# Hyena filter and maxout FFN: the filter's hidden units placed over all four 64x64 quarters of the array, and the first loop's tail reordered

## The chip, the cores and the metric

The kernel runs on one core of one Trainium2 chip. The metric is the device time of one execution in microseconds. The kernel before took 2319.61 us as the median of three runs (2316.99 to 2319.65). One more execution was profiled: it took 2315.53 us, and the profile spans 2313.7 us of it, from the first to the last instruction. All times of single steps below are from that profile, counted from the start of its span.

## The reference

Two blocks follow one another. The first forms a long filter from position embeddings and convolves it, by FFT, with the product of two inputs; the second is a maxout feed-forward network over every token.

```python
# block 1: batch 4, seq S = 12544, d_model 128, filter_order 64
h_mlp  = np.maximum(pos_emb @ w1, 0.0) @ w2      # (S,64)@(64,64), Relu, @(64,128)
h_filt = h_mlp * np.exp(-0.01 * np.arange(S))[:, None]
u = x * v
y = irfft(rfft(u, 2S) * rfft(h_filt, 2S), 2S)[:, :S]
attn = x * y
# block 2: 50176 tokens, d_ff 768
h   = maximum(maximum(t @ w1, t @ w2), t @ w3)   # t: the tokens of attn
out = h @ w_out
```

The window exp(-0.01 n) is zero in float32 beyond 82 x 128 positions, so only the first 82 blocks of 128 positions of the filter are computed (NH = 82, HH = 41).

## The kernel before, in words

The sequence is seen as 98 blocks of 128 positions. The transform is done in two steps: a matmul over the blocks (tables `f1q` for the inputs, `f1h` for the filter), then one over the 128 positions within a block. `NK` = 45 pairs of frequencies follow. Everything is float32. In the profile, one float32 matmul instruction leaves two records, each with its own weight load.

**Start.** Loads of the position embeddings (`posT`, into the memory that `specH` uses later), of `w1` and of small tables are issued on three queues. Meanwhile TensorE multiplies zeros (`warm_up`), and `window_back` (L306) turns the window around into `winr`.

**Relu units of the filter** (`mlp_in`, L318, and `mlp_out`, L329). 82 blocks of positions are held as two halves of 41: half h = 0 on partitions 0 to 63 of `pos`, half h = 1 on partitions 64 to 127. For a position within the block, `mlp_in` multiplies the 41 columns of a half (the stationary operand, 41 columns that stand 128 floats apart in memory) with `w1` (64 wide). The result of half h goes to PSUM partitions 64h to 64h + 40. So half 0 always works in the upper left quarter of the array (rows and columns 0 to 63) and half 1 in the lower right one. Sixteen positions make one call: eight even ones (r = 0, PSUM bank 0 of the tile) and then eight odd ones (r = 1, bank 1). Eight calls alternate between two PSUM tiles `pms`; after each, VectorE takes two instructions (L332) for Relu times window into `hs`, which lies in `spec`.

**First transforms** (`quad`, L847, through `first_halves`, L158). 16 quads transform the 64 filter units from `hs` with `f1h`, whose rows 0 to 40 and 64 to 104 hold the two halves of the table; 32 quads transform the input of the first batch. VectorE converts FFN weights beside them.

**The first loop** (L970). 48 steps pipeline the second transform of filter and batch 0, their product and the inverse transform; step s works on frequency pair s in `g_second`, s - 1 in `s_filter` and `g_swap`, s - 2 in `g_re`, `g_im`, `g_unfold`, and s - 3 in `g_third`. `g_third` ends with a copy by ScalarE (L569) and a store to the DRAM tile `zd` (L570). In the two steps after the last `g_second`, `u_first` (L400) starts the first transform of batch 1 for units 0 to 3, two calls for each unit, each with 16 records on TensorE, one ScalarE copy (L418) and two VectorE instructions (L420). After the loop come `fold` (L913: one transpose of a piece of `w_sb[0]` by TensorE, a copy by ScalarE, and two matmuls into `pl`) for six pieces, `u_turn` for units 4 and 5, and `u_first` for units 4 and 5.

**The FFN** then begins: `t_load` (L642) loads `zt` from `zd` on SyncE's queue, VectorE forms sums (L670, L671), `t_last` (L678) makes the tokens, and `up` and `down` run the FFN, with the convolution of the next batch spread in between. SyncE's queue is in order: in front of the first `zt` load stand the loads of `f4p` (L1022) and `sign` (L1024). Their tiles lie in memory that the pools of the first part held, and the `f4p` load waits until those are free. `eye` and `w_sb[0]`, which the folds read, are in the pool `pin` with `specH` and `w2x`.

Each engine takes its instructions in the order in which the program lists them.

Of the kernel before, what the change touches and what calls it, by code (L numbers as in the profile page):

```python
# [10 lines left out]
FP32 = mybir.dt.float32  # L11
# [5 lines left out]
P = 128  # L17
# [8 lines left out]
N1 = 90  # L26
NH = 82
HH = NH // 2
# [14 lines left out]
def tables(NB):  # L43
    S = P * N1
    k1 = np.arange(N1).reshape(2, N1 // 2).T.ravel()
    n = np.arange(NB)
    a = e(np.outer(n, k1 + 0.25) / N1)
    f1 = np.concatenate([a.real, a.imag], 1)
    up = e(np.outer(n + 0.5, k1 + 0.25) / N1)
    f1q = np.stack([np.concatenate([up.real, up.imag], 1), f1], 1)  # L50
    f1h = np.zeros((64 + HH, 2 * N1))
    f1h[:HH], f1h[64:] = f1[:HH], f1[HH:NH]
    f4 = np.stack([a.T.real, a.T.imag], 1) / S
    f4p = f4[::2].transpose(1, 0, 2).reshape(N1, NB // 2, 2).transpose(0, 2, 1)
    f4 = np.stack([up.T.real, up.T.imag], 1) / S
    f4s = f4[::2].transpose(1, 0, 2).reshape(N1, NB // 2, 2).transpose(0, 2, 1)
    f4q = np.stack([f4p, f4s * np.array([1, -1])[:, None]], 1)
    j, t = np.arange(64), np.arange(64)
    tw = (k1[:, None, None] + 0.25) / S
    half = []  # L60
    for r in range(2):
        s2 = (127 - 2 * t - r)[None, :, None]
        half.append(stacked(e(tw * s2 + j[None, None, :] * s2 / 128)))
    fwd = np.stack(half, 2)
    half = []
    for q in range(2):
        s2 = (2 * t + q)[None, None, :]
        half.append(stacked(e(-tw * s2 - j[None, :, None] * s2 / 128)))
    inv = np.stack(half, 2)
    both = np.stack([fwd, inv], 2)  # L70
    both = both.reshape(N1 // 2, 2, P, 2, 256).transpose(0, 2, 3, 1, 4)
    both = both.reshape(N1 // 2, P, 2, 512)
    j, t = np.arange(32), np.arange(32)
    quarter = [[], []]
    for v in range(2):
        for w in range(2):
            s2 = (63 - 2 * t - v)[None, :, None]
            quarter[0].append(stacked(e(tw * s2 + (2 * j + w)[None, None, :] * s2 / 128)))
            s2 = (2 * t + w)[None, None, :]
            quarter[1].append(stacked(e(-tw * s2 - (2 * j + v)[None, :, None] * s2 / 128)))  # L80
    quarter = np.stack([np.stack(q, 1) for q in quarter], 1)
    quarter = quarter.reshape(N1 // 2, 2, 2, 2, 2, 64, 64).transpose(0, 3, 5, 2, 1, 4, 6)
    quarter = quarter.reshape(N1 // 2, P, 2, 256)
    steps = np.zeros((N1 // 2 + LATE, P, 2, 256))
    steps[:N1 // 2, :, 0], steps[LATE:, :, 1] = quarter[:, :, 0], quarter[:, :, 1]
    f32 = np.float32
    return tuple(np.ascontiguousarray(t, f32) for t in (f1q, f1h, f4q, both, steps))
# [3 lines left out]
def kernel(  # L91
# [15 lines left out]
    nc = tc.nc  # L107
# [50 lines left out]
    def first_halves(ps, lhs, table, dst, copy):  # L158


        for i, a in enumerate(lhs):
            for r in range(2):
                for c in range(2):
                    nc.tensor.matmul(  # L164
                        ps[64 * c:64 * c + 64, 256 * i + r * N1:256 * i + (r + 1) * N1],
                        a[:, r, :], table[:, c * N1:(c + 1) * N1],
                        start=(i % 2 == 0 and r == 0), stop=True, skip_group_check=True)
        copy(dst, ps[:].rearrange("p (s m) -> p s m", m=256)[:, :, 0:2 * N1].rearrange(
            "p s (r k) -> p k r s", r=2))
# [76 lines left out]
    inp = ctx.enter_context(tc.tile_pool(name="inp", bufs=3))  # L246
    utp = ctx.enter_context(tc.tile_pool(name="utp", bufs=2))
    pro = ExitStack()
    pin = pro.enter_context(tc.tile_pool(name="pin", bufs=1))
    eye = pin.tile([P, P], FP32, name="eye")  # L250
    w_sb[0] = pin.tile([D, DFF], FP32, name="w_sb0")
    lwp = pro.enter_context(tc.tile_pool(name="lwp", bufs=3))
    fin = ExitStack()
    inp0 = fin.enter_context(tc.tile_pool(name="inp0", bufs=3))
# [12 lines left out]
    w2_in = sml.tile([P, D], FP32, name="w2_in")  # L267
    w2x = pin.tile([P, D], FP32, name="w2x")
    win = sml.tile([64 + HH, P], FP32, name="win")
    winT = sml.tile([P, 64 + HH], FP32, name="winT")  # L270
    winr = sml.tile([64 + HH, 2, 64], FP32, name="winr")
    back = sml.tile([P, 2, 64], FP32, name="back")
    f1h = sml.tile([64 + HH, 2 * N1], FP32, name="f1h")
    warm = sml.tile([P, 256], FP32, name="warm")
    nc.vector.memset(warm[:], 0.0)
    nc.vector.memset(win[:], 0.0)
# [18 lines left out]
    nc.gpsimd.dma_start(w2_in[0:FO], w2[:, :])  # L295
    nc.gpsimd.dma_start(w2_in[FO:P], w2[:, :])
    nc.gpsimd.dma_start(f1q[:], f1_d)
    nc.scalar.copy(winT[:, 0:64], warm[:, 0:64])

    def warm_up(n):  # L300

# [4 lines left out]
    def window_back():  # L306
        pw = fps.tile([P, 1024], FP32, tag="cv", name="pw", bufs=2)
        nc.tensor.transpose(pw[:, 0:64 + HH], win[:], eye[0:64 + HH, 0:64 + HH])
        nc.scalar.copy(winT[:], pw[:, 0:64 + HH])
        nc.tensor.matmul(pw[0:64 + HH, 512:512 + P], winT[:],  # L310
                         back[:].rearrange("p r t -> p (r t)"), start=True, stop=True)
        nc.scalar.copy(winr[:].rearrange("n r t -> n (r t)"), pw[0:64 + HH, 512:512 + P])

    def w2_order():
# [3 lines left out]
    def mlp_in(i):  # L318

        ps = pms[i % 2]  # L320
        for r in range(2):
            for q in range(8):
                for h in range(2):
                    nc.tensor.matmul(  # L324
                        ps[64 * h:64 * h + HH, 512 * r + q * FO:512 * r + (q + 1) * FO],
                        posv[64 * h:64 * h + 64, P - 1 - 2 * (8 * i + q) - r, :],
                        w1_sb[64 * h:64 * h + 64], start=(q == 0), stop=True,
                        skip_group_check=True)
# [518 lines left out]
    def quad(lhs, table, dst):  # L847
        ps = fps.tile([P, 1024], FP32, tag="cv", name="ps1")
        first_halves(ps, lhs, table, dst, nc.scalar.copy)
# [16 lines left out]
    mps.close()  # L866
    fps = fin.enter_context(tc.tile_pool(name="fps", bufs=4, space=PSUM))
    for f in range(0, FO, 4):
        quad([hs[:, f + i] for i in range(4)], f1h[:], specH[:, :, :, f:f + 4])
        u, k = divmod(f // 4, 4)  # L870
        if u < 2:
            if k in (0, 1):
                u_mul(2 * u + k)
            if k == 2:
                turn2(2 * u)
                for v in range(2 * u + 6, 2 * u + 8):
                    u_load(0, v)
        some(2 if u < 2 and k < 2 else 3)
    wf = {g: load_dir(g, 0) for g in range(3)}
    wi = {g: load_dir(g, 1) for g in range(3)}  # L880
    for u in range(0, NU, 2):
        t = uts.pop(u)
        for v in range(2):
            if u + 4 < NU:
                u_mul(u + 4 + v)
            at = 4 * (u + v)
            quad([t[:, 4 * v + i] for i in range(4)], f1, spec[:, :, :, at:at + 4])
            some(1)
        if u + 4 < NU:
            turn2(u + 4)  # L890
        for v in (u + 10, u + 11):
            if v < NU:
                u_load(0, v)
        some(2)
# [25 lines left out]
    def s_minus(g):  # L920

        m = cvp.tile([P, 2, FO], FP32, tag="minus", name="minus", bufs=1)
        nc.gpsimd.tensor_single_scalar(m[:], specH[:, 2 * g:2 * g + 2, 0], -1.0, op=ALU.mult)
        minus[g] = m
# [41 lines left out]
    loads = dict(zip((NK - 16, NK - 14, NK - 12, NK - 9, NK - 8, NK - 4), range(EARLY)))  # L966
    muls = dict(zip((NK - 13, NK - 11, NK - 10, NK - 5, NK - 3, NK - 1), range(EARLY)))
    turns = {NK - 9: 0, NK - 4: 2}
    s_minus(0)
    for s in range(NK + 3):  # L970
        if s < NK:
            ws[s, 0] = wf[s]
            s_second(s)
            if s + 1 < NK:
                s_minus(s + 1)
            g_second(s)
            wf.pop(s)
            if s + 3 < NK:
                wf[s + 3] = load_dir(s + 3, 0)
        if 1 <= s <= NK:  # L980
            g_swap(s - 1)
            s_filter(s - 1)
        if s >= 3:
            ws[s - 3, 1] = wi.pop(s - 3)
            g_third(s - 3)
            if s < NK:
                wi[s] = load_dir(s, 1)
        if 2 <= s <= NK + 1:
            g_re(s - 2)
            g_im(s - 2)  # L990
            g_unfold(s - 2)
        if s < NK:
            g_butterfly(s)

        if s in muls:
            u_mul(muls[s])
        if s in turns:
            u_turn(turns[s])
            u_turn(turns[s] + 1)
        if s in loads:  # L1000
            u_load(1, loads[s])
        if NK <= s < NK + 2:
            for v in range(4):
                u_first(2 * (s - NK) + v // 2, 2 * (v % 2), 2)
    folded = [fold(0)]
    u_turn(4)
    u_turn(5)
    for f in range(1, NF):
        folded.append(fold(f))
        folded.pop(0)()  # L1010
    folded.pop()()
    nc.scalar.copy(lin[:], pl[:, 0:D])
    for u in (4, 5):
        for h in range(2):
            u_first(u, 2 * h, 2)
    pro.close()


# [153 lines left out]
```

## Time and profile before

| What (us of the span) | before |
|---|---|
| runs: median (lowest to highest) | 2319.61 (2316.99 to 2319.65) |
| span of the profiled execution | 2313.7 |
| TensorE busy, share of the span | 2277.5, 98% |
| `mlp_in` on TensorE, 512 records | 19.2 to 39.3 |
| first record of the filter's quads | 40.8 |
| last `g_third` on TensorE | 314.09 to 316.07 |
| `f4p` load issued / first `zt` load issued | 320.83 / 321.80 |
| first VectorE sum on `zt` | 326.44 |
| stretches at half clock | about 19.4 to 22.8, 313.0 to 316.4, 326.7 to 333.5 |

A line of the profile's groups names the line of the code, the engine, the operation, output and inputs by the program's names, the shapes, and the count; then come busy time, mean duration in nanoseconds, and the idle time of the engine in front of those instructions with what ended it. PE is TensorE's matmuls, PEld its weight loads, DVE VectorE, ACT ScalarE, POOL GpSimd; a name with q is an engine's queue for DMAs. The chain of waits goes back from the last instruction, at each step to what released it. TensorE's ends are modelled: what is measured well is the rate at which records follow each other.

### The profile page before, as it was taken

What the parts mean: (1) busy time and instruction counts of PE and PEld (TensorE: products, weight loads), DVE (VectorE), ACT (ScalarE), POOL (GpSimd) and SP (SyncE); (2) the same over time, 40 slices, a digit from 0 to 9 for tenths busy, and PEclk for the clock granted to TensorE, in tenths of its full rate; (3) what the DMA queues carried; (4) which work ended last, traced back from release to release, by engine and by line L of the source; (5) the groups of instructions that cost most, each with busy time, mean ns of one, the idle gap of its engine ahead of it and who ended that gap; (6) DMA issues with size and microseconds to landing.
All of it is one profiled execution on the core that took longest, in us unless ns stands there. A gap on an engine that the chain in (4) does not pass through costs nothing.

```text
span 2313.7 us, 68365 instructions
## 1 busy us (share of the span) xinstructions
PE 2277.5 (98%) x27853; PEld 1379.8 (60%) x27853; DVE 1574.2 (68%) x2856; ACT 1177.5 (51%) x2124; POOL 898.8 (39%) x1095
## 2 busy tenths in 40 slices
PE   8999989999999999999999999999999999999998
PEld 7989866655555546655555446655555546666665
DVE  5678856667887847757888847758888854445443
ACT  2678844446666624446666634446666632222222
POOL 1045424413333324423333333423333326666666
PEclk9999999999999999999999999999999999999999
DMA  7869959979998849979999849969999832222221
GB/s 158 206 202 266 290 155 189 166 172 246 232 244 216 210 119 192 185 147 242 248 243 250 214 120 189 186 144 247 247 246 240 225 91 56 54 56 71 65 55 22
DMA packets 473148, 410.95 MB, mean 178 GB/s; under 512 B 328004, under 2 KB 374231, under 8 KB 472834
## 3 DMA queue, kind: packets, MB, share of 16 engines
q1 hardware_dynamic: 433714, 317.68, 62.4%
q0 software_dynamic: 26400, 75.72, 11.2%
q10 hardware_dynamic: 12720, 13.18, 1.8%
q8 instruction: 219, 3.59, 0.7%
q14 instruction: 95, 0.78, 0.1%
HBM read 262.77 MB, written 84.67 MB: 150 GB/s over the span
## 4 chain that ended last, share of the span: by engine, by line
PE 84%; DMA 6%; ACT 3%; DVE 3%; issue 2%; SPq 1%; ACTq 1%; POOL 0%; DVEq 0%; POOLq 0%
PE hps L155 41%; PE ops L155 17%; PE ops L765 6%; PE cps L409 5%; PE cps L155 4%; PE cps L463 3%; PE ps L164 3%; PE cps L473 2%; DMA ht<-hd 2%; PE last L155 1%; DMA hd<-ht 1%; ACT ht L958 1%; DMA wt<-wq_const 1%; PE pm L324 1%; DMA zt<-zd 1%
## 5 line engine op out<-in xcount | busy, mean ns | idle before, releaser
L155 PE MATMUL hps<-gt,w_sb 128*64 128x392 f32 x6144 | 1150.4, 495 | 6.1 <-DVE hid L705 5.3
L702 ACT ACTIVATE hid<-hps 128x392 f32<-128x392 f32 x768 | 383.9, 500 | 736.6 <-PE hps L155 720.7
L155 PEld LDWEIGHTS hps<-gt,w_sb 128*64 128x64 f32 x6144 | 424.5, 137 | 437.4 <-issue 391.3
L705 DVE TENSOR_TENSOR hid<-hid,hps 128x392 f32<-128x392 f32 x768 | 427.3, 557 | 333.6 <-PE hps L155 323.9
L155 PE MATMUL ops<-hid,wo_sb 128*64 128x392 f32 x2304 | 478.6, 492 | 0.0
L515 POOL TENSOR_TENSOR cb<-cb,xs 128x512 f32<-128x512 f32 x135 | 181.7, 1346 | 471.4 <-DVE xs L512 331.1
L155 PEld LDWEIGHTS ops<-hid,wo_sb 128*64 128x64 f32 x2304 | 169.0, 137 | 210.2 <-issue 210.2
L488 DVE TENSOR_TENSOR cb<-cps,eo 128x512 f32<-128x512 f32 (+1 forms) x288 | 175.1, 649 | 65.6 <-ACT eo L485 65.1
L420 DVE TENSOR_TENSOR spec<-cps,high 128x360 f32<-128x360 f32 x180 | 135.5, 794 | 121.9 <-ACT high L418 121.9
L720 POOL DMA_DIRECT2D out_dram<-ot x96 | 74.9, 781 | 354.2 <-ACT ot L718 301.8
L503 ACT ACTIVATE xs<-cb 32x512 f32<-32x512 f32 x270 | 169.6, 628 | 22.8 <-DVE cb L488 14.3
L504 ACT COPY xs<-cb 32x512 f32<-32x512 f32 x270 | 166.3, 616 | 3.1
L418 ACT COPY high<-cps 128x360 f32<-128x360 f32 x90 | 71.9, 799 | 152.5 <-PE cps L409 125.8
L519 DVE TENSOR_TENSOR xs<-cb 128x256 f32<-128x256 f32 x270 | 141.8, 568 | 7.5 <-POOL cb L515 7.5
L409 PEld LDWEIGHTS cps<-f1q,uT 98*64 98x64 f32 x2880 | 124.9, 137 | 30.6 <-issue 30.6
L409 PE MATMUL cps<-f1q,uT 98*64 98x90 f32 x2880 | 128.1, 241 | 0.4 <-DVE uT L393 0.4
L378 POOL COPY planes<-ut 128x784 uint16<-128x784 uint16 x90 | 75.7, 841 | 111.1 <-DVE ut L357 110.2
L496 POOL DMA_DIRECT2D zd<-cb x135 | 92.5, 687 | 61.9 <-DVE cb L488 54.0
L155 PEld LDWEIGHTS cps<-f4p,even 90*64 90x64 f32 x1568 | 89.8, 139 | 38.4 <-issue 34.7
L155 PE MATMUL cps<-f4p,even 90*64 90x49 f32 x1568 | 96.5, 221 | 2.8 <-DVE even L670 2.8
L155 PE MATMUL cps<-f4p,zt 90*64 90x49 f32 x1568 | 97.8, 223 | 0.3 <-DVE zt L671 0.3
L507 DVE TENSOR_TENSOR cb<-cb,ht 128x512 f32<-128x512 f32 x135 | 92.0, 682 | 7.7 <-ACT xs L504 7.1
(137 smaller groups left out, 3205.9 us busy)
## 6 DMA issues: line engine op xcount, KB each, us to landing
ht<-hd SPq DMA_DIRECT2D x264, 256.0 KB, 6.8
wt<-wq_const SPq DMA_DIRECT2D x144, 256.0 KB, 6.4
zd<-cb POOLq DMA_DIRECT2D x135, 256.0 KB, 6.1
zt<-zd SPq DMA_DIRECT2D x384, 90.0 KB, 3.0
sq<-spec SPq DMA_DIRECT2D x264, 128.0 KB, 7.3
ut<-in_xr_dram SPq DMA_DIRECT2D x128, 196.0 KB, 4.2
ut<-in_vr_dram SPq DMA_DIRECT2D x128, 196.0 KB, 4.5
xT<-in_x_dram SPq DMA_DIRECT2D x256, 98.0 KB, 3.5
```

Of the source, the lines that this page charges most:

```text
L155: nc.tensor.matmul(out[64 * h:64 * h + 64], lhsT[:, 64 * h:64 * h + 64], rhs, start=start, stop=stop, skip_group_check=True)
L409: nc.tensor.matmul(ps[64 * c:64 * c + 64, 256 * i + h * N1:256 * i + (h + 1) * N1], t[:, 2 * ((at + i) % 8) + h].rearrange("n r t -> n (r ...
L420: nc.vector.tensor_tensor(out=spec[:, :, a, at:at + n], in0=v[:, 1], in1=high, op=op)
L488: nc.vector.tensor_tensor(out=cb[:, a, lo:hi], in0=ps[:, lo:hi], in1=eo[:, lo:hi], op=op)
L496: nc.gpsimd.dma_start(zd[b][2 * z:2 * z + 2].rearrange("k c t a f -> (k c t) a f"), zss.pop(z))
L503: nc.scalar.mul(xs[at:at + 32], xt[at + 32:at + 64], -1.0)
L504: nc.scalar.copy(xs[at + 32:at + 64], xt[at:at + 32])
L515: nc.gpsimd.tensor_tensor(out=xts[g], in0=xts[g], in1=xs[:], op=ALU.add)
L519: nc.vector.tensor_tensor(out=ab[:, q], in0=y[:, 0], in1=y[:, 1], op=(ALU.subtract, ALU.add)[q])
L702: nc.scalar.activation(h[:], pa[:, 0:N], Relu)
L705: nc.vector.tensor_tensor(out=h[:], in0=h[:], in1=pb[:, 0:N], op=ALU.max)
L765: nc.tensor.matmul(ps[64 * c:64 * c + 64, 0:H2], w, rhs[:, H2 * c:H2 * c + H2], start=start, stop=True, skip_group_check=True)
```

## The change

In `mlp_in` the loop over r moves inside the loop over q, and half h of odd positions (r = 1) goes to column group 64 (1 - h): the four matmuls of a pair of positions now lie in all four quarters. In the odd positions the two halves of the blocks therefore stand exchanged in PSUM and in `hs`. The table `f1h` gets a second version with its halves exchanged, used for r = 1 (147.7 KB in place of 73.8 KB); `first_halves` takes a pair of tables; `winT` gets a second version too, made by four copies in place of one and multiplied by two matmuls in place of one.

In the first loop's tail, the folds move into the loop: two in step 45, two in step 46, the last two after the turns of units 4 and 5. `u_first` of units 0 and 1 moves from step 45 to the end of step 46, and that of units 2 and 3 from step 46 to after the loop. `eye` and `w_sb[0]` get a pool of their own, `raw0`, opened ahead of `pin`.

```diff
-    f1h = np.zeros((64 + HH, 2 * N1))
-    f1h[:HH], f1h[64:] = f1[:HH], f1[HH:NH]
+    f1h = np.zeros((64 + HH, 2, 2 * N1))
+    f1h[:HH, 0], f1h[64:, 0] = f1[:HH], f1[HH:NH]
+    f1h[:HH, 1], f1h[64:, 1] = f1[HH:NH], f1[:HH]
...
-                        a[:, r, :], table[:, c * N1:(c + 1) * N1],
+                        a[:, r, :], table[r][:, c * N1:(c + 1) * N1],
...
+    raw0 = pro.enter_context(tc.tile_pool(name="raw0", bufs=1))
+    eye = raw0.tile([P, P], FP32, name="eye")
+    w_sb[0] = raw0.tile([D, DFF], FP32, name="w_sb0")
     pin = pro.enter_context(tc.tile_pool(name="pin", bufs=1))
-    eye = pin.tile([P, P], FP32, name="eye")
-    w_sb[0] = pin.tile([D, DFF], FP32, name="w_sb0")
...
-        nc.scalar.copy(winT[:], pw[:, 0:64 + HH])
-        nc.tensor.matmul(pw[0:64 + HH, 512:512 + P], winT[:],
-                         back[:].rearrange("p r t -> p (r t)"), start=True, stop=True)
+        for r in range(2):
+            for h in range(2):
+                c = 64 * (h ^ r)
+                nc.scalar.copy(winT[:, r, c:c + HH], pw[:, 64 * h:64 * h + HH])
+        for r in range(2):
+            nc.tensor.matmul(pw[0:64 + HH, 512 + 64 * r:576 + 64 * r], winT[:, r], back[:, r],
+                             start=(r == 0), stop=True, skip_group_check=True)
...
-        for r in range(2):
-            for q in range(8):
+        for q in range(8):
+            for r in range(2):
                 for h in range(2):
+                    c = 64 * (h ^ r)
                     nc.tensor.matmul(
-                        ps[64 * h:64 * h + HH, 512 * r + q * FO:512 * r + (q + 1) * FO],
+                        ps[c:c + HH, 512 * r + q * FO:512 * r + (q + 1) * FO],
...
+    drain = {NK: [lambda: folding(0), lambda: folding(1), lambda: folded.pop()()],
+             NK + 1: [lambda: folding(2), lambda: folding(3), lambda: folded.pop()(),
+                      lambda: unit(0), lambda: unit(1)]}
...
-        if NK <= s < NK + 2:
-            for v in range(4):
-                u_first(2 * (s - NK) + v // 2, 2 * (v % 2), 2)
-    folded = [fold(0)]
+        for job in drain.get(s, ()):
+            job()
     u_turn(4)
     u_turn(5)
-    for f in range(1, NF):
-        folded.append(fold(f))
-        folded.pop(0)()
+    folding(4)
+    folding(5)
     folded.pop()()
     nc.scalar.copy(lin[:], pl[:, 0:D])
-    for u in (4, 5):
-        for h in range(2):
-            u_first(u, 2 * h, 2)
+    for u in range(2, 6):
+        unit(u)
```

More of the change, by code (lines that the diff above doesn't have):

```diff
@@ L269 @@
     win = sml.tile([64 + HH, P], FP32, name="win")
-    winT = sml.tile([P, 64 + HH], FP32, name="winT")
+    winT = sml.tile([P, 2, 64 + HH], FP32, name="winT")
     winr = sml.tile([64 + HH, 2, 64], FP32, name="winr")
     back = sml.tile([P, 2, 64], FP32, name="back")
-    f1h = sml.tile([64 + HH, 2 * N1], FP32, name="f1h")
+    f1h = sml.tile([64 + HH, 2, 2 * N1], FP32, name="f1h")
     warm = sml.tile([P, 256], FP32, name="warm")
@@ L297 @@
     nc.gpsimd.dma_start(f1q[:], f1_d)
-    nc.scalar.copy(winT[:, 0:64], warm[:, 0:64])
+    for r in range(2):
+        nc.scalar.copy(winT[:, r, 0:64], warm[:, 0:64])
     def warm_up(n):
@@ L320, in mlp_in @@
         ps = pms[i % 2]
-        for r in range(2):
-            for q in range(8):
+        for q in range(8):
+            for r in range(2):
                 for h in range(2):
+                    c = 64 * (h ^ r)
                     nc.tensor.matmul(
-                        ps[64 * h:64 * h + HH, 512 * r + q * FO:512 * r + (q + 1) * FO],
+                        ps[c:c + HH, 512 * r + q * FO:512 * r + (q + 1) * FO],
                         posv[64 * h:64 * h + 64, P - 1 - 2 * (8 * i + q) - r, :],
@@ L868 @@
     for f in range(0, FO, 4):
-        quad([hs[:, f + i] for i in range(4)], f1h[:], specH[:, :, :, f:f + 4])
+        quad([hs[:, f + i] for i in range(4)], (f1h[:, 0], f1h[:, 1]), specH[:, :, :, f:f + 4])
         u, k = divmod(f // 4, 4)
@@ L886 @@
             at = 4 * (u + v)
-            quad([t[:, 4 * v + i] for i in range(4)], f1, spec[:, :, :, at:at + 4])
+            quad([t[:, 4 * v + i] for i in range(4)], (f1, f1), spec[:, :, :, at:at + 4])
             some(1)
@@ L968, with folding, unit @@
     turns = {NK - 9: 0, NK - 4: 2}
+    folded = []
+    def folding(f):
+        folded.append(fold(f))
+        if len(folded) > 1:
+            folded.pop(0)()
+    def unit(u):
+        for h in range(2):
+            u_first(u, 2 * h, 2)
+    drain = {NK: [lambda: folding(0), lambda: folding(1), lambda: folded.pop()()],
+             NK + 1: [lambda: folding(2), lambda: folding(3), lambda: folded.pop()(),
+                      lambda: unit(0), lambda: unit(1)]}
     s_minus(0)
```

## Prediction

> **What bounds the kernel now.** I read the page's busy shares first, then the chain of waits, then timelines of the two stages that the change touches. TensorE carries the span, and the chain agrees:
>
> ```profile
> PE 2277.5 (98%) x27853; PEld 1379.8 (60%) x27853; DVE 1574.2 (68%) x2856; ACT 1177.5 (51%) x2124; POOL 898.8 (39%) x1095
> ...
> PE 84%; DMA 6%; ACT 3%; DVE 3%; issue 2%; SPq 1%; ACTq 1%; POOL 0%; DVEq 0%; POOLq 0%
> ```
>
> So a microsecond taken from a stretch where TensorE's own order sets the pace reaches the end, if nothing later has a fixed start. The first 60 us of the chain (pieces: start, length, what) show that `mlp_in` is such a stretch, with the quads right behind it:
>
> ```profile
> 14.39 4.78 DMA ut<-in_xr_dram
> ...
> 19.22 20.06 PE pm L324 x512
> ...
> 40.84 3.94 PE ps L164 x96
> ```
>
> It starts when the position embeddings have landed (its loads wait for all eight; the chain names a neighbour). From there to 120 us TensorE is over 97% busy and every load of the quads is gated by TensorE or VectorE, so an earlier end moves all of it. Within the stage, a table of stretches (length, PE, PEld, clock, DMA):
>
> ```profile
> 19.40:22.80 3.40, 3.40 (x66) 3.38 (x67) 0.50 1.14 258
> 24.00:38.00 14.00, 14.00 (x392) 14.00 (x390) 1.00 0.46 100
> ```
>
> At half clock a record takes 53.3 ns, at full clock 36.3 (VectorE's pairs come every 2.32 us, and 64 records lie between). Halving the clock doubles a pace that the array sets; here 1.47. Something else sets it at full clock. VectorE isn't it:
>
> ```profile
> 27.68 1.29 DVE L332 SCALAR_TENSOR_TENSOR spec<-pm,winr 105x512 f32<-105x512 f32 x2 [1.04 <-PE pm L324]
> 30.00 1.29 DVE L332 SCALAR_TENSOR_TENSOR spec<-pm,winr 105x512 f32<-105x512 f32 x2 [1.03 <-PE pm L324]
> ```
>
> It waits 1.03 of every 2.32 us. The second stage, in the chain:
>
> ```profile
> 308.93 0.60 DVE spec L420 x2
> 309.53 0.60 DVE xt L545
> ...
> 312.91 1.46 PE ps L409 x16
> 314.37 1.72 PE ps L155 x16
> ...
> 320.42 0.27 PE pt L915
> ...
> 320.83 0.38 SPq L1022
> ...
> 321.80 0.99 SPq L646
> 322.84 3.52 DMA zt<-zd
> ```
>
> `g_re` of the last pair follows `u_first`'s VectorE work, the last `g_third` follows `u_first` on TensorE, and the first `zt` load follows the `f4p` load, which waits for the last fold's transpose. Then `zt`'s landing ends TensorE's idle time (324.3 to 327.2).
>
> **What the Trainium skill says.** "TensorE: Matmul & The Clock Gate", section "LDWEIGHTS (loading the stationary operand)", prices a weight load by columns, P / 1.2 ns. The trace agrees in slope: 105 columns (L310) take 167 to 171 ns, 64 columns 133 to 137: 34 ns for 41 columns, 0.83 each. By that, 41 columns would take about 112. But:
>
> ```profile
> L324 PEld LDWEIGHTS pm<-w_sb,specH x512: 144/163/192, 19.2 to 39.0; 64*41 64x41 f32 x171
> ```
>
> The minimum is 144. "SBUF — State Buffer", section on the DMA port swizzle, says that accesses that each cross to a new 16-byte line pay a penalty. These columns stand 512 bytes apart, so 32 ns more, 66 in place of 34, fits; no other stationary operand here is strided, so only this row shows it. The same TensorE page, Part 3, says that a load overlaps running matmuls only in other row groups. The trace differs: in the quads (L164, all rows) a record follows every 38.7 ns in two column groups, 77.4 for each, which is 90 columns in two passes at 2.4 GHz (75) and nothing for the load. Part 1 gives the clock windows, 3413 ns, free-running; the stretches above fit, and a window in which TensorE was under about half busy (0.18 of 3.4 us at 16.0, 1.63 at 309.6, 1.03 at 323.2) is followed by one at half clock.
>
> **Reading of the 36.3.** In the tokens' matmuls (90x49, two column groups, loads of 64 columns) groups of four records follow at 0.115 us, 57.5 for two, although 49 columns stream in 41: that is one load (53.3) and 4 ns, with both column groups loading at once. For `mlp_in` the same form gives 66 to 68 and 4: 72.6 for two, as measured. At half clock the streaming of 64 columns (107) hides it. So a quarter is paced by its own strided load, and two quarters are idle.
>
> **The change part by part.**
> (1) `mlp_in`. Same 256 matmuls, 512 records. With four quarters loading side by side, four records per 72.6 ns: 18.2 each, 1.16 us a call; in half clock 107 / 4 = 26.7 each, 1.71. The four-quarter form exists in L953 (128 columns, four records every 109 ns), so the array does it; whether two strided loads from the same partitions run at once, no row shows. Bounds: not at all (36.3 stays), or fully (18.2). I take fully, because the tokens' loads do so from the same partitions. Then VectorE sets the pace: a buffer's round is 1.16 + 0.2 matmul latency + 1.29 + 0.15 of handoffs, 2.8 us for two calls, 1.4 a call against 2.32. Call 0 and 1 at half clock end at 22.7 (now about 23.8), six more by VectorE bring its last instruction to 32.6, against 40.6: 8.0. No row packs records closer than L953's 27 ns; as a floor that is 1.74 a call, an end at 34.7 and 5.9. I take 7.2.
> (2) Tables and window. 74 KB more on GpSimd's queue, issued at 3.9 while the DMA engines are full (0.99 to 1.11): at 214 GB/s 0.35 us at most on the embeddings' landing, nothing at least; 0.2. Three more ScalarE copies at 0.25 and one matmul: the window is needed at 23.1 and is ready at 14.6, so nothing. Quads keep their count.
> (3) Drain. In the built program the `f4p` load now waits for `s_filter`'s last matmul (303.2) and not for the last fold (320.4), so it and `sign` are out of the way. From 302.14: `g_third`(42) to 304.3, two transposes, then TensorE is held by the folds' copies, which stand behind the `ht` copy (to 305.3), the `zs` copy and its store (306.2): copies to 306.8, matmuls to 307.2. `g_third`(43) to 308.2 (now 309.2). VectorE's chain for pair 44 runs at once, 305.4 to 308.1 (now 309.4 to 312.3). Folds 2 and 3 wait for copies to 309.9 and end at 310.3; four halves of `u_first` at 0.66, with PSUM slots freed by VectorE, to 313.0; the last `g_third` 313.0 to 314.1, now 316.1. Copy 0.6, store issue 0.4, landing 3.4 (the store's median), then `zt` issue and landing 4.6 as now: 322.9. But TensorE, ScalarE and VectorE still have turns, two folds and eight halves: they start at 317.4 and go on by VectorE at 0.68 each, so VectorE is free at 324.0. The first sum is at 324.0 against 326.4: 2.4. The tokens and first FFN steps now lose about 2.5 us to half clock up to 333.5; whether a window falls under half busy again is open (the wait for VectorE leaves 1.9 us idle), so I add 0.8. Bounds: 0 (folds holding TensorE in step 45 can bring a half-clock window too) to 6; I take 3.2.
> Sum: -7.2 + 0.2 - 3.2 = -10.2 us, a span of 2303.5. The profiled execution ran 4 us under the median of the runs; on the median 2309.4.
>
> **Rivals.**
> A. Loads of the same rows take turns, because a strided load holds the partitions' read port. Then 36.3 stays at full clock; only the half-clock stretch gains: 94 records in place of 64 in 3.41 us, 30 at 36.3 = 1.1. For it: loads and line crossings are what sets the pace, and both quarters of a half read the same partitions. Against: the tokens' loads. Time: -1.1 + 0.2 - 3.2 = -4.1, 2315.5: within what can't be told.
> B. The quarters work, but the drain gives nothing: the folds' waits and another half-clock window take back 2.4. -7.0: 2312.6.
> C. Slower: two strided loads on one row group disturb each other, so that each costs more than 72.6 in turn. 256 loads per row group: at 110 ns 28.2 us against 18.6, +9.6; with +0.2 - 3.2 it is +6.6, 2326. It decides from 102 ns. Against: nothing in the trace shows loads in conflict.
>
> **How the numbers follow.** Forecast 0.61, A 0.21, B 0.10, C 0.08. Likeliest 2309.5, its own range 2305 to 2313. A and B lie inside 2304.5 to 2317.5; C and the tails are left out. 0.2% is 4.6 us, about what runs of this kernel can tell. Faster by more: nearly all of the forecast, B, and little of A: 0.70; within: most of A and edges, 0.21; slower: C and a little, 0.09.
>
> **What would show it.** Step 1: VectorE's pairs 1.3 to 1.6 us apart, idle time before L332 under 2 us in all, the first quad near 33. If 2.32 apart, A; above, C. Step 2: first `mlp_in` record at 19.2 to 19.6. Step 3: `f4p` issued before the last `g_third`, the first `zt` sum about 9.5 us earlier than 326.4, and behind VectorE's `u_first` work, not behind a DMA. If the stage is short but the end isn't, later steps have a fixed start, and I am wrong on both.

## The result, and the profile after

The changed kernel took 2310.38 us as the median of six runs (2308.97 to 2312.90), the kernel before 2318.81 in the six runs beside it (2315.85 to 2322.14). The ratio is 0.9965, with a 95% interval of 0.9952 to 0.9978. The medians are 8.4 us apart; the interval says between 5.1 and 11.1. The changed kernel's median lies 0.9 us above the predicted 2309.5. The profiled execution spans 2308.4 us, 5.3 less than the 2313.7 before, where the prediction's sum said 10.2 less. So the forecast was met in the runs, and the steps behind it only in part.

Busy times on the page after: TensorE's matmuls are busy for 7.2 us less and its weight loads for 10.8; the other engines changed by 2.4 us at most.

```profile
PE 2270.3 (98%) x27855; PEld 1369.0 (59%) x27855; DVE 1575.3 (68%) x2856; ACT 1179.9 (51%) x2128; POOL 899.7 (39%) x1095
```

The chain of waits from `mlp_in` to the end of the first quads (start, length, what):

```profile
19.20 10.08 PE pm L332 x357
29.27 1.09 issue
30.37 3.46 PE pm L332 x120
33.83 0.27 issue
34.09 0.59 PE pm L332 x12
...
36.25 5.59 PE ps L165 x96
41.85 1.01 PE pst L370 x8
```

The stage starts where it did (19.20, before 19.22). The first quad follows at 36.25 in place of 40.84: 4.6 us gained. But two pieces called "issue" (time in which TensorE waited for nothing that the profile shows), 1.09 and 0.27 us, stand inside the stage, where the kernel before had none; and the first 96 records of the quads take 5.59 us, before 3.94, which gives 1.65 back. At the second quad 2.9 us are left. VectorE's timeline (start, busy, line, operation; in brackets the idle time in front and what ended it) shows calls 1.6 us apart until the first pause holds VectorE up for 1.84 us:

```profile
23.09 1.37 DVE L340 SCALAR_TENSOR_TENSOR spec<-pm,winr 105x512 f32<-105x512 f32 x2 [0.30 <-PE pm L332]
24.67 1.29 DVE L340 SCALAR_TENSOR_TENSOR spec<-pm,winr 105x512 f32<-105x512 f32 x2 [0.21 <-PE pm L332]
26.43 2.71 DVE L340 SCALAR_TENSOR_TENSOR spec<-pm,winr 105x512 f32<-105x512 f32 x4 [0.47 <-PE pm L332]
30.98 2.78 DVE L340 SCALAR_TENSOR_TENSOR spec<-pm,winr 105x512 f32<-105x512 f32 x4 [1.84 <-PE pm L332]
```

Stretches of the span (length, then busy time and count of PE, PEld, DVE, ACT, POOL; clock; DMA share; GB/s):

```profile
19.46:22.80 3.34, 3.34 (x127) 3.34 (x126) 1.29 (x2) 0.00 (x0) 0.00 (x0) 0.50 1.21 252
23.00:29.20 6.20, 6.20 (x246) 5.97 (x243) 5.23 (x8) 0.00 (x0) 0.00 (x0) 1.00 1.24 254
33.10:36.50 3.40, 1.55 (x50) 1.30 (x44) 2.46 (x5) 0.00 (x0) 0.00 (x0) 1.00 0.00 0
36.60:39.90 3.30, 3.30 (x49) 3.30 (x47) 3.16 (x10) 0.76 (x1) 0.13 (x1) 0.50 0.02 5
```

At half clock a record takes 3.34 / 127 = 26.3 ns, half of the 53.3 before, as predicted. At full clock it takes 6.20 / 246 = 25.2, hardly less: the array isn't what sets this pace. The last two lines are the 1.65 us: the stage now ends in a window in which TensorE is busy for 1.55 of 3.40 us, and the next 3.4 us, the first quads, run at half clock.

The drain. SyncE's queue (start, length), and the end of the chain:

```profile
300.56 0.38 SPq L1040 DMA_DIRECT2D f4p<-f4p_const  x1
...
313.89 1.88 SPq L654 DMA_DIRECT2D zt<-zd  x2
```

```profile
311.00 0.60 ACT zs L577
...
319.58 0.60 DVE spec L428 x2
...
320.45 0.34 DVE spec L428
320.79 0.60 DVE even L678
```

`f4p` is issued 20.3 us earlier, the first `zt` load 7.9 us earlier, and the first sum (L678), before at 326.44 behind a DMA, now begins at 320.7 behind VectorE's work of `u_first`. By then the changed kernel is 5.7 us ahead, at the FFN's first record 6.5 (323.94 against 330.40). Counted from the FFN's first `ops` record, behind the half-clock stretches at its start, 6.6 us are left; from there to the end 1.3 of them are lost, most of it in one wait of 1.2 us for a convolution table near 1060 us (experiments 9 to 11).

### The profile page after: what moved, and what is told of

Read it like the earlier page. It is cut to its first block, busy times and chain, and to the rows that moved or that the text cites. A ratio compares the mean times of both kernels' runs of the same rounds, so it can differ in the third digit from the quotient of the medians.

```text
span 2308.4 us, 68374 instructions
## 1 busy us (share of the span) xinstructions
PE 2270.3 (98%) x27855; PEld 1369.0 (59%) x27855; DVE 1575.3 (68%) x2856; ACT 1179.9 (51%) x2128; POOL 899.7 (39%) x1095
## 3 DMA queue, kind: packets, MB, share of 16 engines
q8 instruction: 219, 3.59, 0.7%
## 4 chain that ended last, share of the span: by engine, by line
PE 83%; DMA 7%; ACT 3%; DVE 3%; issue 2%; SPq 1%; ACTq 0%; POOL 0%; DVEq 0%; POOLq 0%
PE hps L156 40%; PE ops L156 17%; PE ops L773 6%; PE cps L417 5%; PE cps L156 4%; PE ps L165 3%; PE cps L471 3%; PE cps L481 2%; DMA wt<-wq_const 2%; DMA ht<-hd 2%; DMA hd<-ht 2%; PE last L156 1%; ACT ht L966 1%; PE pst L370 1%; DMA zt<-zd 1%
```

## The experiments

Comparisons of a few us inside one profile are made from the starts of records. Between kernels, half-clock stretches fall differently in each execution, and a reading that met one says so. "The FFN's start" is its first `ops` record here.

**1. The quarters alone** (`quarters_only`): the changed kernel with the first loop's tail and its pool as before.

```diff
-        for job in drain.get(s, ()):
-            job()
+        if NK <= s < NK + 2:
+            for v in range(4):
+                u_first(2 * (s - NK) + v // 2, 2 * (v % 2), 2)
... (folds, turns, u_first(4), u_first(5) and the pool as in the kernel before)
```

> The four quarters in mlp_in, with the first loop's tail and its pool as before. My theory (the two parts add up, read from the stages of the two profiles): Relu units end 4.6 us earlier than before, a half-clock window in the quads takes back 1.65, so the first loop's last s_filter comes 2.5 to 3.5 us earlier and the run is 0.10 to 0.17% faster than before (2.5 to 4 us). Rival (the drain's gain needs the earlier quarters' part, or the whole gain is the drain's): no faster than before by more than 0.05%.

Median 2313.66 of eight runs, the kernel before 2317.93 of 22; ratio 0.998 [0.997, 0.999], 2.3 to 7.0 us faster. The stage ran from 19.19 to 34.88, again with pauses after the same records:

```profile
25.98 3.46 PE pm L331 x118
29.44 1.36 issue
30.81 3.46 PE pm L331 x119
34.26 0.27 issue
34.54 0.59 PE pm L331 x12
```

Its profile was 2.5 us ahead at the second quad, and 1.8 at the last `s_filter`, where 2.5 to 3.5 were expected. That it was 2.7 ahead at the FFN's start comes from the drain: the kernel before met half clock there and this profile did not (the table under experiment 8). It lost 3.0 later. So the first part has an effect by itself, and the two pauses belong to it.

**2. The drain alone** (`tail_only`): before's `mlp_in`, the drain and the pool `raw0` of the changed kernel.

```diff
+    raw0 = pro.enter_context(tc.tile_pool(name="raw0", bufs=1))
...
-        if NK <= s < NK + 2:
-            for v in range(4):
-                u_first(2 * (s - NK) + v // 2, 2 * (v % 2), 2)
+        for job in drain.get(s, ()):
+            job()
```

> The tail of the first loop reordered and the pool split, with mlp_in as before. My theory: the first sum on zt comes 2.4 to 3 us earlier against s_filter's last start, and with less half clock at the FFN's start the run is 3 to 4.5 us faster, 0.13 to 0.19%. Rival (clock windows decide: what the tail gains is lost where another window falls to half clock): under 2 us, 0.08%.

Median 2316.45 of 14 runs; ratio 0.9996 [0.9986, 1.0005]: 0.9 us, not told from nothing; under 2 us, as the rival had it, and not the theory's 3 to 4.5. In its profile the drain did what it should: 1.4 us behind the kernel before at the last `s_filter` (its quads had met a half-clock stretch), 2.0 ahead at the FFN's start. The table under experiment 8 has a likely reason why so little of it shows in the runs.

**3. Filling the gaps** (`filled_both`): the changed kernel with multiplications of no use where TensorE waits, three rounds behind the last `mlp_out` and three at the drain's end.

```diff
         mlp_out(i - 1)
+    warm_up(3)
...
+    for _ in range(3):
+        halves_mm(pf[:, 0:256], wo_sb[:, 0, :],
+                  wo_sb[:, 0:2, :].rearrange("p c d -> p (c d)"), True, True)
```

> The changed kernel with matmuls on dummy data in two idle stretches of TensorE: three warm_up pairs after the last mlp_out, and three pairs at the end of the tail. If the half-clock windows at 36.5 and 323.2 come from those idle stretches, both vanish: the first 96 records of the quads take 3.9 us and not 5.6, the first 24 records of the FFN about 4 us and not 5.5; 2 to 3 us in all, 0.10 to 0.13% below the changed kernel. Rival (the windows follow something else, or the fillers delay the work behind them): both windows stay and the time is that of the changed kernel within 0.05%.

The window that was 1.55 us busy now is 3.06, and no half-clock stretch follows; the quads' first 96 records take 3.94 again:

```profile
33.00:36.40 3.40, 3.06 (x62) 2.11 (x59) 2.47 (x5) 0.00 (x0) 0.00 (x0) 1.00 0.00 0
```

So the half-busy window is what brought the 1.65 us. The FFN's first 24 records, too, take 4.17 us in place of 5.49, as expected. The runs don't show the gain: 2309.66 (five runs), ratio 0.9966 [0.9953, 0.9979], as the changed kernel. The profile has a new half-clock stretch in the drain, 301.7 to 308.5, behind this window in which TensorE waits for the folds' copies:

```profile
298.30:301.70 3.40, 1.15 (x18) 0.92 (x20) 2.82 (x6) 1.93 (x4) 1.04 (x2) 1.00 0.77 187
```

**4. Both column groups from the same rows** (`same_rows`): the kernel before, with both halves read from partitions 0 to 63; half of the filter's blocks is computed from the wrong positions.

```diff
-                        posv[64 * h:64 * h + 64, P - 1 - 2 * (8 * i + q) - r, :],
-                        w1_sb[64 * h:64 * h + 64], start=(q == 0), stop=True,
+                        posv[0:64, P - 1 - 2 * (8 * i + q) - r, :],
+                        w1_sb[0:64], start=(q == 0), stop=True,
```

> mlp_in of before, but both column groups take their stationary and moving operand from partitions 0 to 63, so half 1 of the filter units is computed from the positions of half 0. This measures whether two strided weight loads from the same partitions run side by side. If they do, the record pace at full clock stays at 36.3 ns and mlp_in at 20 us. Rival (loads of the same rows take turns): 68 to 73 ns a record, mlp_in about 35 us.

Inconclusive at full clock, since the whole stage ran at half clock, 53.3 ns a record:

```profile
19.10:53.10 34.00, 32.17 (x574) 32.00 (x576) 15.07 (x30) 0.76 (x1) 1.10 (x2) 0.50 0.35 78
```

Two records in 106.7 ns is the pace of the kernel before at half clock, so two loads from the same rows fit into it; had they taken turns at 72.6 each, 145 would be needed. That speaks against rival A and doesn't measure the loads.

**5 and 6. A stationary operand without a stride** (`two_packed`: the kernel before; `four_packed`: the changed one). 41 neighbouring columns are loaded; positions are wrong, the array's work is the same.

```diff
-                        posv[64 * h:64 * h + 64, P - 1 - 2 * (8 * i + q) - r, :],
+                        pos[64 * h:64 * h + 64, HH * (2 * (8 * i + q) + r):HH * (2 * (8 * i + q) + r + 1)],
```

> The kernel before with mlp_in's stationary operand read as 41 neighbouring columns of the embeddings in place of 41 columns that stand 512 bytes apart; these are the wrong positions, the work on the array is the same. Theory (a quarter is paced by its own strided load): a contiguous load of 41 columns should be near 112 ns for a matmul, 56 a record, so with 4 ns about 60 for a record of each of two quarters, 30 ns a record at full clock in place of 36.3; VectorE's pairs 1.9 to 2.0 us apart. Rival (the rate at which instructions are supplied or started sets the 36.3): 36.3 stays and the pairs stay at 2.32.

> The changed kernel with the same contiguous stationary operand (wrong positions, same work on the array). Theory (with four quarters the strided loads lie side by side and no longer set the pace; 25 ns a record is the rate at which TensorE is given instructions): 24 to 26 ns a record at full clock, the two pauses of about 1.1 and 0.3 us after records 371 and 499 as in the changed kernel, last record at 34.2 to 35.0. Rival (the strided loads still set the 25, by taking turns in part): 14 to 19 ns a record, then VectorE sets 1.4 us a call and the stage ends near 32.6.

The first calls' operands come from the loads that land first, so both stages start at 16.3; no later load is among what TensorE waited for in them. The weight loads of `mlp_in` in four kernels at full clock (count, then shortest, median and longest in ns): before, after, `two_packed`, `four_packed`:

```profile
L324 PEld LDWEIGHTS pm<-w_sb,specH x390: 162/163/165, 23.8 to 38.0; 64*41 64x41 f32 x195
```

```profile
L332 PEld LDWEIGHTS pm<-w_sb,specH x243: 155/196/209, 22.9 to 29.0; 64*41 64x41 f32 x122
```

```profile
L324 PEld LDWEIGHTS pm<-w_sb,specH x512: 110/114/115, 16.3 to 33.5; 64*41 64x41 f32 x171
```

```profile
L332 PEld LDWEIGHTS pm<-w_sb,specH x512: 110/114/192, 16.3 to 33.5; 64*41 64x41 f32 x171
```

The stride costs 49 ns a load with one load per row group (163 for 114), and 82 with two (196). In the forms without it, 114 stays 114 with four quarters. The pace between pauses is 27.9 ns in `two_packed` and 14.0 in `four_packed`: the first theory holds, and of the second pair of expectations the rival's pace does, though not its end of the stage near 32.6. The 25 ns of the changed kernel are strided loads that lengthen each other; TensorE can start records in half of that. And yet `four_packed` isn't faster. TensorE's timeline in it:

```profile
16.27 1.87 PE L332 MATMUL pm<-w_sb,specH 64*41 64x64 f32 x116
20.01 1.32 PE L332 MATMUL pm<-w_sb,specH 64*41 64x64 f32 x76 [1.87 <-issue]
21.82 0.98 PE L332 MATMUL pm<-w_sb,specH 64*41 64x64 f32 x52 [0.50 <-DVE spec L340]
24.29 1.31 PE L332 MATMUL pm<-w_sb,specH 64*41 64x64 f32 x76 [1.48 <-issue]
26.10 0.98 PE L332 MATMUL pm<-w_sb,specH 64*41 64x64 f32 x52 [0.50 <-DVE spec L340]
29.11 1.37 PE L332 MATMUL pm<-w_sb,specH 64*41 64x64 f32 x76 [2.03 <-issue]
```

and in `two_packed`:

```profile
16.33 3.54 PE L324 MATMUL pm<-w_sb,specH 64*41 64x64 f32 x118
20.32 3.77 PE L324 MATMUL pm<-w_sb,specH 64*41 64x64 f32 x128 [0.45 <-issue]
24.60 3.77 PE L324 MATMUL pm<-w_sb,specH 64*41 64x64 f32 x128 [0.50 <-issue]
29.70 4.10 PE L324 MATMUL pm<-w_sb,specH 64*41 64x64 f32 x138 [1.33 <-issue]
```

Each pause marked "issue" comes 128 records after the one before it, and the stretch from resuming to resuming is 4.1 to 5.1 us in both, whatever the array could do: 4.28, 4.82, 4.10 and 4.28, 5.10. From the first record's start to the last one's they need 17.3 us; the changed kernel, with a slower array but a later start, 15.2. (`four_packed` met half clock from 30.2 on. That delays its last record by some 0.2 us: the records in front of the last pause are slower, but the pause's end is set by the next block.) Their single runs took 2310.11 and 2313.52, the kernel before 2318.65 in the one run beside them. 128 records are 256 instructions, a matmul and a weight load each. The list of DMA queues has what supplies them:

```profile
q8 instruction: 219, 3.59, 0.7%
```

219 transfers for 2 x 27855 = 55710 instructions of TensorE are 254 each, and 3.59 MB over 219 are 16.4 KB. So this is TensorE's instruction stream in blocks of 256. The Trainium skill, "Runtime: NRT & Kernel Launch", section "Instruction fetch mechanics", describes such blocks and calls the cost of a boundary "mostly hidden". Here it is not: in the trace of the changed kernel block transfers start at 27.74 and 31.47, take 1.15 and 1.30 us, and TensorE resumes 2.6 us after each start. Full DMA engines are not the reason: from 31.4 to 34.1 their share is 0.03. What fills the rest of the 2.6 us is not shown.

**7. Moving the boundary** (`warm_longer`): the changed kernel with 56 more of TensorE's instructions, 28 records, ahead of the stage.

```diff
-    warm_up(3)
+    warm_up(10)
```

> The changed kernel with ten rounds of the multiplications by zero in place of three ahead of mlp_in: 28 more matmuls, 56 more instructions or 28 records, in time in which TensorE waits for the embeddings. Theory (the pauses in mlp_in come where a block of 256 instructions ends and the next has not landed): both pauses move 28 records earlier, to after records 343 and 471. Rival (they come from VectorE's buffers or from a fixed time): they stay after 371 and 499, or at 29.3 and 33.8 us. Clock: if a window with TensorE under half busy brings the half clock, the stretch at 19.4 to 22.9 vanishes, and the first 66 records take 1.7 us in place of 3.4; the stage ends about 1.2 us earlier unless the pauses take it back.

```profile
19.39 5.56 PE L332 MATMUL pm<-w_sb,specH 64*41 64x64 f32 x215
25.52 3.38 PE L332 MATMUL pm<-w_sb,specH 64*41 64x64 f32 x128 [0.57 <-issue]
29.80 3.37 PE L332 MATMUL pm<-w_sb,specH 64*41 64x64 f32 x128 [0.90 <-issue]
33.80 1.21 PE L332 MATMUL pm<-w_sb,specH 64*41 64x64 f32 x41 [0.64 <-issue]
```

The pauses stand after records 343 and 471, each 28 earlier, and a third appears at 215 = 243 - 28. With TensorE busy ahead of the stage the half-clock stretch at 19.4 is gone, but the stage still takes 15.4 us: what the clock gives, the pauses take. So the pauses belong to the instruction stream, which bounds the stage together with the strided loads, and the other halves of the expectations (VectorE's buffers, a fixed time) are out. The single run, 2315.80, lost 4.1 us after the FFN's start.

**8. The drain without the new pool** (`tail_no_pool`): `eye` and `w_sb[0]` back in `pin`.

```diff
-    eye = raw0.tile([P, P], FP32, name="eye")
-    w_sb[0] = raw0.tile([D, DFF], FP32, name="w_sb0")
...
+    eye = pin.tile([P, P], FP32, name="eye")
+    w_sb[0] = pin.tile([D, DFF], FP32, name="w_sb0")
```

> The changed kernel with eye and w_sb[0] back in the pool of specH, the order of the drain as changed. The f4p load then waits for the last fold, at about 312 to 313 us. Theory (after the reordering the first zt load waits for the store of the last g_third's copy, which lands later than that): the first zt load is issued at the same distance from the last zs copy as in the changed kernel, within 0.5 us, and the first FFN step starts as in the changed kernel. Rival (the separate pool is what brings zt forward): zt issued at least 2 us later, and the FFN start later too.

```profile
316.34 0.38 SPq L1039 DMA_DIRECT2D f4p<-f4p_const  x1
...
317.39 1.88 SPq L653 DMA_DIRECT2D zt<-zd  x2
```

The last `zs` copy started at 314.27, so the first `zt` load comes 3.12 us after it, in the changed kernel 2.89. As expected the pool gives 0.2 us at most (the `f4p` load itself came at 316.34, not at 312 to 313). But the FFN didn't start as in the changed kernel: 3.3 us later, and the trace has half clock from 306.1 to 312.9. All thirteen profiles (those of experiments 9 to 11 too) sort by this alone. Time from the last `s_filter` record to the first sum:

| order of the drain | no half clock in it | 3.4 us | 6.8 us |
|---|---|---|---|
| before | 22.24, 22.37, 22.54 | 23.46, 23.49 | |
| changed | 20.60, 20.61, 20.86 | 21.89, 22.06 | 22.82, 22.96, 23.16 |

The means at full clock are 22.38 and 20.69: the order is worth 1.7 us. A stretch of 3.4 us at half clock costs 1.1 to 1.3, one of 6.8 costs 2.3. `tail_no_pool` is the 22.82, inside its group: nothing is left for the pool. The changed order met such a stretch in five of eight profiles, the old one in two of five. Over all of them the means are 22.82 and 21.87, 0.95 apart.

**9 and 10. Both kernels once more** (`after_again`, `before_again`), unaltered.

> The changed kernel unaltered, a second profile. Theory (mlp_in is bound by blocks of instructions; half-clock windows and the landing of loads in the later convolutions differ from one execution to the next): the pauses come again after records 371 and 499; against the first profile of the kernel before, the first quad is 4 to 5.5 us earlier, the first FFN step 2 to 7 us earlier depending on where half-clock stretches fall between 300 and 335 us, and the distance from there to the end differs from the first profile's by up to 2 or 3 us. Rival (the later loss of 1.3 us is a fixed property of the changed kernel): the same loss, at the same place near 1060 us.

> The kernel before unaltered, a second profile. Theory: mlp_in takes 19.8 us from first to last record again, without a pause; its later waits for loads differ from the first profile's 0.3 us, between 0 and 4 us, since its runs spread over 7 us although the first profile was among the shortest. Rival (the kernel before meets no such waits, the changed one does): 0.3 us or less again.

The spans were 2309.0 and 2314.2: 5.2 apart, the first two 5.3. The pauses of 1.1 and 0.3 us came after records 371 and 499 again, and before's 19.9 us without one. The half clock in the quads was 6.8 us long this time: of 4.4 us at the first quad 1.2 were left at the second (44.43 against 45.63), and 2.6 at the last `s_filter`. The later loss of 1.3 us against the first profile of the kernel before didn't come back, so it isn't fixed. The changed kernel still waited 0.7 us for its tables between 900 and 1800 us (1.9 the first time), the kernel before 0.3 us both times; that its longer runs meet more is not shown.

**11. Tables loaded earlier** (`early_weights`): the changed kernel.

```diff
-            at(s - 4, 0, w_load, x)
+            at(s - 6, 0, w_load, x)
...
-    wp = conv.enter_context(tc.tile_pool(name="wp", bufs=3))
+    wp = conv.enter_context(tc.tile_pool(name="wp", bufs=4))
```

> The changed kernel with the convolution tables' loads (wt) two steps further ahead, and a fourth buffer for them. Theory (some executions lose 1 to 4 us where a batch begins, near 1060 and 1650 us, because wt lands behind other loads in SyncE's queue while the DMA engines are full): TensorE's waits for wt disappear from 900 to 1800 us; if nothing takes their place the runs' median falls by 1 to 2 us against the changed kernel's 2310.4, and their spread narrows. Rival (the DMA engines are full there, so that what is loaded earlier delays something else): waits for sq or zt take the place, and the runs stay within 1 us of 2310.4.

TensorE's waits between 900 and 1800 us, in the changed kernel's first profile and here:

```profile
PE hps L156 <- DVE hid L713: 3.3, 6, 0.6
PE cps L471 <- DMA wt<-wq_const: 1.9, 3, 1.2
```

```profile
PE hps L156 <- DVE hid L713: 2.7, 5, 0.5
```

The waits for `wt` are gone and none for another load took their place. One profile doesn't show that the earlier loads did this: `filled_both`, whose loads are as in the changed kernel, had no wait for `wt` either. From the FFN's start to the end this profile gained 0.9 us on the kernel before, where the changed kernel's lost 1.3 and 0.0. The runs: 2308.55 (five, 2307.35 to 2313.41), the kernel before 2316.24 (nine); ratio 0.9966 [0.9952, 0.9979]. It is faster than before, and can't be told from the changed kernel; the spread did not narrow. The 2313.41 is its profiled run, which met 6.8 us of half clock in the drain.

## Why the prediction was right, and where not

*Start (step 2).* Predicted 0.2 us later, at 19.2 to 19.6: 19.20, nothing lost.

*`mlp_in` (step 1).* Predicted 7.2 us; the first quad is 4.6 earlier. The direction is right: the quarters do load side by side, so A and C are out (C would need 102 ns for every load in turn; four records, two for each row group, take 101 ns together). At half clock the pace is as predicted. Two terms are wrong. First, TensorE's pace at full clock: "four records per 72.6 ns" assumed that two strided loads from the same rows cost no more than one. They take 196 ns in place of 163, and a record 25.2 in place of 18.2; a call is 1.6 us, TensorE stays the slower side, and VectorE never sets the 1.4. The written floor of 27 ns a record came near this pace, for another reason; its end at 34.7 is that of VectorE's last instruction, which ended at 36.0. Second, the instruction stream was not in the sum at all: 1.36 us of pauses. It hid in the profile before: a block lasted 128 x 36.3 ns = 4.65 us there, about what a block needed from resuming to resuming in the profiles with pauses (3.7 in the changed kernel, 4.0 to 5.1 in experiments 5 to 7). The transfers started at 25.96, 30.15 and 33.97 there, and TensorE reached these blocks at 29.37, 34.02 and 38.67, so each had more than the 2.6 us. Of the signs named, the pairs of VectorE are 1.6 apart, at the upper end; its idle time is 3.8 us in place of under 2, and the first quad stands at 36.25 in place of near 33. (The "now about 23.8" for the second call is a misreading: VectorE takes that call at 25.35. The sum doesn't use it.)

*Behind the stage.* "An earlier end moves all of it" missed that the shorter stage ends in a less busy window: 1.65 us lost to half clock in the quads. The rule on half-busy windows was in the prediction's text, and applied to the drain only. Of 7.2 us, 2.9 reached the second quad.

*Drain (step 3).* Predicted 3.2 us to the FFN's first steps; measured from the second quad to the FFN's first record 3.5 (from 2.9 us ahead to 6.5). The order of events came as written: `f4p` out of the way, `zt` early, the first sum behind VectorE's `u_first`. The schedule written for the changed drain was good to 0.4 us: a first sum at 324.0, measured 320.7 with 2.9 already gained ahead of it, so 323.6. But the difference of 2.4 (measured 2.8) was counted from a profile of the kernel before that had 3.4 us of half clock in its drain, worth 1.1; at full clock in both, the order gives 1.7 us. From the first sum to the FFN's first record it gained 0.7, where 0.8 was added. The bound "folds holding TensorE in step 45 can bring a half-clock window too" came true in five profiles of eight, and there most or all of the gain is lost: rival B's mechanism, part of the time. (B's own sum of -7.0 takes back the whole 3.2, not the 2.4 in its text.) The 0.95 us over all profiles agrees with the 0.9 of `tail_only` in the runs; that half clock is what cost those runs the rest is likely, not shown.

*The sum.* In the two pairs of profiles 5.3 and 5.2 us, in the runs 8.4 by the medians with an interval down to 5.1. That the median agrees with 2309.5 is partly luck: 7.2 us were counted for step 1 and 2.9 arrived, and the runs of the kernel before lie some 3 us further above its profiled execution than those of the changed kernel above its own (3.3 and 0.2 by the medians, counted from 2315.53 and 2310.21). Part of that may be the sample: the kernel before's median was 2317.93 in the 22 runs and 2316.24 in the nine runs beside the experiments, 7.6 and 5.9 above 2310.38, and the profiled execution of `before_again`, 2315.99, lies at the median of those nine. What makes some of its runs longer stays open.

## What to carry to other kernels

When a stage of small matmuls is made denser, ask what else has a pace near the old one: here the stream of instructions, 256 in 3.7 to 5.1 us, stood right behind the strided loads, and neither faster loads (`four_packed`) nor a higher clock (`warm_longer`) shortened the changed stage. Fewer, larger instructions may; that was not tried. And a stage that gets shorter changes how busy the clock's windows are: price the window behind its end, not only the stage.

## What the runs showed of the hardware beyond that

- A strided stationary operand (64 x 41, 512 bytes apart) loads in 163 ns in place of 114, and in 196 when a second one from the same rows loads beside it; contiguous ones stay at 114 with four quarters at work.
- TensorE paused for 0.3 to 2.0 us at the ends of most blocks of 256 of its instructions in stages that could go through a block in 1.8 to 3.6 us (128 records at 14.0 to 27.9 ns), and did not where a block lasted 4.65 us.
- With only rows 0 to 63 in use (`same_rows`) the clock stayed at half for 34 us, though TensorE was busy for 32.17 of 34.00 us. Why is open; nothing was tried on it.
- What came ahead of half clock, in windows counted from the ends of the half-clock stretches in the first 340 us of the thirteen profiles: at full clock, a window of 3.41 us with TensorE busy for less than 1.55 us was followed by half clock each time, one with more than 1.83 us never; in between both occurred. At half clock it took more: windows with up to 2.66 us kept the next one at half, those from 2.71 on ended the stretch. `same_rows` does not fit this, nor does one window of `after_again` (3.13 us).
